# Input loads of a fused convolution and two-layer kernel, split at a multiple of 16 rows

## The chip, the cores and the metric

The kernel runs on one core of a Trainium2 chip. The time is that of the device for one execution, in microseconds (us); where several runs were made, their median is given. The profile is one execution, recorded instruction by instruction, in us from the start of its span.

## What is computed

```python
def _attn_ref(x, weight):
    ...
    w = np.exp(weight - max); w = w / sum          # 8 heads, 7 taps
    x_pad = np.concatenate([zeros(B, 6, D), x], axis=1)
    out = np.einsum('hk,bskhg->bshg', w, x_unf)    # causal 7-tap average, one set of taps per head

def _moe_ref(x, w_in, w_out):
    h = x @ w_in
    g = np.maximum(0.01 * h, h)
    return g @ w_out

def _moe2_ref(x, w_in, w_out, a, b):
    h = x @ w_in
    P = a[0] + a[1]*h + a[2]*h**2 + a[3]*h**3
    Q = 1.0 + abs(b[0])*abs(h) + abs(b[1])*h**2
    return (P / (Q + 1e-06)) @ w_out
```

`x` is 2 x 4096 rows of 192 float32. The convolution's result goes through the first layer (192 to 2048 to 192) and then the second, 8192 rows in all. The four weight matrices arrive as float64 (read as pairs of 32-bit words).

## The kernel before

The 8192 rows are cut into 16 blocks of 512. For each block the kernel loads rows of `x` into one of two tiles `xt` (alternating), forms the convolution on TensorE with banded matrices made of the taps (`conv`), evacuates it to `xc`, transposes it, and splits it in a high and a low part (`xh`, `xl`). Layer 1 runs 16 steps of 128 hidden columns, each with five matrix products into a bank and five into the accumulators `acc`; layer 2 does the same with the rational function between. The two layers of neighbouring blocks are interleaved.

A block is loaded as NTC = 5 overlapping chunks of CR = 109 rows, each 103 rows further on; the last chunk has 106 rows. A row is 768 B. `load_x` issues this as two transfers on SP: L415 takes the full chunks (`109x4x192`), L418 the last (`106x192`). The first block of each half (blocks 0 and 8) begins with six rows of zeros, so its first chunk is a transfer of 103 rows of its own (L411), and L415 has three chunks.

The weights come in 28 pieces through three buffers `raw` (L333, L337 for `w_in`, L339 for `w_out`; 384 or 512 KB each), and each piece is converted by ACT, DVE and POOL from float64 words to a high and a low float32 part. A piece can be loaded only when the piece that had its buffer has been converted: its last reader is `cv_bits`, two `scalar_tensor_tensor` on DVE. Pieces called "m" and "r" belong to `w_in`, those called "o" to `w_out`. The pieces of an "r" kind go through one more pair of SBUF-to-SBUF transfers on SP (`r_dup`, L391).

At the start the taps are normalised on ACT and DVE, stored to DRAM (`s_put`, L302), and read back as bands (`s_get`, L307); DVE and ACT copy them to `band` (L313, L219), and only then can the first convolution run.

The order of all instructions on each engine is fixed when the kernel is built: a planner (`Planner.run`) lists every step with an estimated cost and writes the instructions engine by engine. `load_x` counts there as one step on SP with the cost of three transfers, whatever it issues. All transfers of the kernel, loads, stores (L601) and copies, are issued by SP, in that one order. Each transfer takes the next of eight completion semaphores (`DMAHW0` to `DMAHW7`) in turn, and where its semaphore was used before, it is issued only when that earlier transfer has landed.

The names that the prediction uses: the raw buffers are raw_126, raw_127 and raw_128; "o1" is the second piece of layer 1's `w_out` (in raw_128), "o2" the third (in raw_126).

Of the kernel before, what the change touches and what calls it, by code (L numbers as in the profile page):

```python
# [16 lines left out]
P = 128  # L17
# [139 lines left out]
def conv_leaky_rational_kernel(  # L157
# [12 lines left out]
    nc = tc.nc  # L170
    B, S, D = x.shape
    H, K = weight.shape
# [5 lines left out]
    CT = -(-FB // NTC)  # L178
    CR = CT + K - 1
# [222 lines left out]
        tt(w, buf[("dup", l, q, half)][R:2 * R], f(w), ALU.subtract)  # L402


    def load_x(eng, i):
        b, s0, n, _ = blocks[i]
        t = xt[i % 2]
        ntc = -(-n // CT)
        first = 1 if s0 == 0 else 0
        if first:  # L410
            nc.sync.dma_start(out=t[K - 1:CR, 0, :], in_=x[b, 0:CT, :])  # L411
        r0 = s0 - (K - 1) + first * CT
        src = bass.AP(tensor=x.tensor, offset=x.offset + (b * S + r0) * D,
                      ap=[[D, CR], [CT * D, ntc - 1 - first], [1, D]])
        nc.sync.dma_start(out=t[0:CR, first:ntc - 1, :], in_=src)  # L415
        r0 = s0 - (K - 1) + (ntc - 1) * CT
        rows = n - (ntc - 1) * CT + K - 1
        nc.sync.dma_start(out=t[0:rows, ntc - 1, :], in_=x[b, r0:r0 + rows, :])  # L418

    def zero_x(eng, i):  # L420
        nc.vector.memset(xt[i % 2][0:K - 1, 0, :], 0.0)
# [189 lines left out]
    t1, t2, t = [], [], 0.0  # L611
# [4 lines left out]
    end1, t = t, LEAD  # L616
    for i in range(NB):
        t = max(t, t1[i * NJ + NJ - 1] + GAP)
# [76 lines left out]
    def prep(i):  # L695
        n = blocks[i][2]
        ntc = -(-n // CT)
        p = i % 2
        base = t1[i * NJ]
        c = [base - PREP + STEP * k for k in range(4)] if i else [-77.0] * 4  # L700
        if i >= 2 and blocks[i][1] == 0:
            on(DVE(0.25), base - 66, 2.0, zero_x, i, w=[("xt", p)])
        on(SP(P * ntc * D * 4, 3), max(base - 66, 4) if i else -80, 2.0, load_x, i, w=[("xt", p)], extra=DMA_LAND)
        for m in range(2):
            cps, xps = ("cps", i, m), ("xps", i, m)
            on(PE(0.774), c[m], 2.45, conv, i, m, r=[("xt", p), ("band", m)], w=[cps], take=("bank", cps))
            on(ACT(t_act(ntc * HC) + (m and t_act(ntc * R))), c[m], 4.35, conv_evac, i, m, r=[cps], w=[("xc", m)])
        for m in range(2):
            xps = ("xps", i, m)
            on(PE(0.11 * ntc), c[2 + m], 2.45, trans, i, m, r=[("xc", 0), ("xc", 1), "ident"], w=[xps],  # L710
               take=("bank", xps))
            src = lambda k=xps: buf[k]
            on(ACT(t_act(n)), c[2 + m], 4.35, x_hi, 0, i, m, src, r=[xps], w=[("xh", 0, m, p)])
            on(DVE(t_dve(n)), c[2 + m], 4.36, x_lo, 0, i, m, src, r=[xps, ("xh", 0, m, p)], w=[("xl", 0, m, p)])
# [120 lines left out]
```

## Time and profile before

| | |
|---|---|
| median of 3 runs | 1354.74 us (1353.61 to 1354.93) |
| the profiled execution | 1353.6 us, its span 1351.8 us |
| TensorE (PE) busy | 1268.9 us, 94% |
| ACT busy | 1212.5 us, 90% |
| DVE busy | 1164.5 us, 86% |
| POOL busy | 1160.8 us, 86% |
| mean granted TensorE clock | 0.972 |
| transfers of `x` | 14 of 327 KB and 2 of 245 KB (L415), 16 of 79.5 KB (L418), 2 of 77 KB (L411) |

The span is the time from the first to the last instruction; 1.8 us of the execution lie around it. An engine's busy share is an average over the whole span: the first 160 us, in which the weights are converted, look unlike the rest. A row of the timeline names the engine's idle time ahead of the instruction in square brackets, and what ended it. SPq is SP's issuing of transfers.

### The profile page before, as it was taken

The page shows a single profiled execution, that of the slowest core. Times are in us where ns is not written, and L with a number is a line of the kernel's source. Part 1 is how long each engine was busy: PE and PEld are TensorE (multiplying, and loading weights), DVE is VectorE, ACT ScalarE, POOL GpSimd, SP SyncE. Part 2 cuts the span into 40 slices and gives each one's busy share as a digit, 9 for nine tenths or more (in the row PEclk, how much of TensorE's full clock was granted, in tenths as well). Part 3 has the DMA queues.
Part 4 walks back from the last instruction along what each step waited for, and adds up shares of the span by engine and source line. Part 5 has one row for each costly group of instructions (what it writes and reads, how often), then busy time and mean ns, then how long its engine had stood idle before and what let it go on. Part 6 is the DMA issues. An engine that isn't in the chain of part 4 may idle for free.

```text
span 1351.8 us, 18187 instructions
## 1 busy us (share of the span) xinstructions
PE 1268.9 (94%) x5722; PEld 1024.6 (76%) x5722; DVE 1164.5 (86%) x1784; ACT 1212.5 (90%) x2258; POOL 1160.8 (86%) x934
## 2 busy tenths in 40 slices
PE   4489699999999999999999999999999999999976
PEld 3367578788888878878888887888888787888754
DVE  3399689989989898988989898898989889898996
ACT  2289599999999999999999999999999999999996
POOL 0157499989999899899999989999998998989997
PEclk6689899999999999999999999999999999999997
DMA  4244200000000000000000000000000000000000
GB/s 118 74 126 124 70 4 1 15 10 5 21 1 25 1 24 1 20 5 15 11 1 25 1 25 1 12 1 17 9 13 13 1 25 1 12 1 12 1 13 13
DMA packets 26312, 29.34 MB, mean 22 GB/s; under 512 B 1674, under 2 KB 23654, under 8 KB 26214
## 3 DMA queue, kind: packets, MB, share of 16 engines
q1 hardware_dynamic: 26214, 28.16, 6.8%
q8 instruction: 45, 0.74, 0.2%
q14 instruction: 53, 0.43, 0.1%
HBM read 19.76 MB, written 6.30 MB: 19 GB/s over the span
## 4 chain that ended last, share of the span: by engine, by line
PE 65%; DVE 13%; ACT 11%; SPq 3%; issue 3%; POOL 2%; DMA 2%; ACTq 0%; DVEq 0%; POOLq 0%
PE bank L228 34%; PE acc L228 30%; ACT work L219 7%; SPq L418 3%; DVE work L225 3%; ACT raw L219 3%; DVE work L222 2%; DVE pair L225 2%; DVE bank L225 2%; DVE raw L225 1%; DVE xl L222 1%; DMA raw<-in_moe_w_out_dram 1%; ACT pair L219 1%; PE bank L577 1%; POOL pair L222 1%
## 5 line engine op out<-in xcount | busy, mean ns | idle before, releaser
L228 PE MATMUL acc<-pair,wo 128*128 128x512 f32 x2560 | 670.1, 397 | 29.3 <-ACT pair L219 21.1
L228 PEld LDWEIGHTS acc<-pair,wo 128*128 128x128 f32 x2560 | 475.1, 189 | 137.7 <-ACT pair L219 22.3
L219 ACT ACTIVATE work<-work 128x512 f32<-128x512 f32 x541 | 339.0, 631 | 22.4 <-DVE work L225 16.3
L222 POOL TENSOR_TENSOR pair<-work,pair 128x512 fp32r<-128x512 f32 x196 | 256.1, 1308 | 82.5 <-ACT pair L219 65.0
L222 DVE TENSOR_TENSOR work<-work,bank 128x512 f32<-128x512 f32 (+1 forms) x393 | 253.1, 657 | 16.6 <-ACT work L219 16.6
L219 ACT ACTIVATE work<-bank 128x512 f32<-128x512 f32 (+2 forms) x406 | 226.7, 565 | 9.4 <-PE bank L228 7.7
L228 PE MATMUL bank<-xh,wiH 128*128 128x512 f32 x512 | 207.7, 406 | 26.2 <-DVE work L222 12.9
L222 POOL TENSOR_TENSOR work<-work,pair 128x512 f32<-128x512 f32 x166 | 215.3, 1299 | 14.8 <-DVE pair L225 5.2
L228 PE MATMUL bank<-xh,wiL 128*128 128x512 f32 x512 | 201.4, 393 | 0.0
L228 PE MATMUL bank<-xl,wiH 128*128 128x512 f32 x512 | 201.1, 393 | 0.0
L228 PE MATMUL bank<-xl,wiR 128*128 128x512 f32 x512 | 200.9, 392 | 0.1
L228 PE MATMUL bank<-xh,wiR 128*128 128x512 f32 x512 | 200.8, 392 | 0.0
L219 ACT ACTIVATE raw<-raw 128x512 f32<-128x512 f32 x242 | 151.6, 630 | 7.6 <-DVE raw L225 5.8
L222 POOL TENSOR_TENSOR pair<-work,work 128x512 fp32r<-128x512 f32 x113 | 146.9, 1301 | 11.5 <-DVE work L225 8.0
L225 DVE SCALAR_TENSOR_TENSOR work<-work,b_sb,bank 128x512 f32<-128x512 f32 x166 | 123.5, 744 | 37.9 <-ACT work L219 36.6
L225 DVE SCALAR_TENSOR_TENSOR pair<-bank,a_sb,work 128x512 fp32r<-128x512 f32 x178 | 132.9, 747 | 18.8 <-ACT work L219 14.7
L228 PEld LDWEIGHTS bank<-xh,wiH 128*128 128x128 f32 x512 | 96.9, 189 | 66.6 <-DVE work L222 20.5
L225 DVE SCALAR_TENSOR_TENSOR work<-bank,a_sb,work 128x512 f32<-128x512 f32 x166 | 123.9, 746 | 12.0 <-POOL work L222 11.0
L225 DVE SCALAR_TENSOR_TENSOR bank<-work,a_sb,bank 128x512 f32<-128x512 f32 x175 | 131.5, 752 | 2.8
L219 ACT ACTIVATE pair<-work 128x512 fp32r<-128x512 f32 x196 | 123.6, 631 | 6.1 <-DVE work L222 5.5
L219 ACT ACTIVATE work<-bank,a_sb 128x512 f32<-128x512 f32 x175 | 119.0, 680 | 4.5 <-PE bank L228 3.3
L222 POOL TENSOR_TENSOR raw<-raw,pair 128x512 f32<-128x512 f32 x90 | 116.9, 1300 | 5.6 <-DVE pair L225 1.9
(80 smaller groups left out, 1912.5 us busy)
## 6 DMA issues: line engine op xcount, KB each, us to landing
raw<-in_moe_w_out_dram SPq DMA_DIRECT2D x16, 384.0 KB
xt<-in_x_dram SPq DMA_DIRECT2D x14, 327.0 KB
out_dram<-work SPq DMA_DIRECT2D x22, 192.0 KB
raw<-in_moe_w_in_dram SPq DMA_DIRECT2D x8, 512.0 KB
raw<-in_moe_w_in_dram SPq DMA_DIRECT2D x8, 256.0 KB
work<-work SPq DMA_DIRECT2D x16, 128.0 KB
out_dram<-raw SPq DMA_DIRECT2D x10, 192.0 KB
xt<-in_x_dram SPq DMA_DIRECT2D x16, 79.5 KB
```

Of the source, the lines that this page charges most:

```text
L219: nc.scalar.activation(out=out_, in_=in_, func=func, **k)
L222: (eng or nc.vector).tensor_tensor(out=out_, in0=in0, in1=in1, op=op)
L225: nc.vector.scalar_tensor_tensor(out=out_, in0=in0, scalar=s, in1=in1, op0=op0, op1=op1)
L228: nc.tensor.matmul(out=out_, lhsT=w, rhs=r, start=start, stop=stop)
L418: nc.sync.dma_start(out=t[0:rows, ntc - 1, :], in_=x[b, r0:r0 + rows, :])
L577: nc.tensor.transpose(ps[:, t * P:(t + 1) * P], src[:, t * P:(t + 1) * P], ident)
```

## The change

The full chunks are now loaded with 128 rows each instead of 109 (the 19 further rows are never read by `conv`, which takes rows 0 to 108). The first chunk of blocks 0 and 8 (103 rows) and the last chunk of every block (106 rows) are each split in a transfer of 96 rows and one of the rest, 7 or 10 rows.

```diff
+    def load_rows(t, p0, chunk, src, rows):
+        even = rows - rows % 16
+        for r0, r1 in ((0, even), (even, rows)):
+            if r1 > r0:
+                nc.sync.dma_start(out=t[p0 + r0:p0 + r1, chunk, :], in_=src[r0:r1, :])
+
     def load_x(eng, i):
...
         if first:
-            nc.sync.dma_start(out=t[K - 1:CR, 0, :], in_=x[b, 0:CT, :])
+            load_rows(t, K - 1, 0, x[b, 0:CT, :], CT)
         r0 = s0 - (K - 1) + first * CT
         src = bass.AP(tensor=x.tensor, offset=x.offset + (b * S + r0) * D,
-                      ap=[[D, CR], [CT * D, ntc - 1 - first], [1, D]])
-        nc.sync.dma_start(out=t[0:CR, first:ntc - 1, :], in_=src)
+                      ap=[[D, P], [CT * D, ntc - 1 - first], [1, D]])
+        nc.sync.dma_start(out=t[:, first:ntc - 1, :], in_=src)
         r0 = s0 - (K - 1) + (ntc - 1) * CT
         rows = n - (ntc - 1) * CT + K - 1
-        nc.sync.dma_start(out=t[0:rows, ntc - 1, :], in_=x[b, r0:r0 + rows, :])
+        load_rows(t, 0, ntc - 1, x[b, r0:r0 + rows, :], rows)
```

The instructions on PE, ACT, DVE and POOL stay as they were, in the same order. On SP there are 18 transfers more, and the lines of `load_x` move: L415 is L421 in the changed kernel, and L411 and L418 are L409.

The start of SP's order, up to the storing of the taps. `raw_126` and `raw_127` are the first two weight pieces, `xt_76` is block 0's tile, `work_103` holds the taps:

```order
 L333 DMA raw_126<-in_moe_w_in_dram 128x1024
 L337 DMA raw_127<-in_moe_w_in_dram 64x1024 x2
-L411 DMA xt_76<-in_x_dram 103x192
-L415 DMA xt_76<-in_x_dram 109x3x192
-L418 DMA xt_76<-in_x_dram 106x192
+L409 DMA xt_76<-in_x_dram 96x192
+L409 DMA xt_76<-in_x_dram 7x192
+L421 DMA xt_76<-in_x_dram 128x3x192
+L409 DMA xt_76<-in_x_dram 96x192
+L409 DMA xt_76<-in_x_dram 10x192
 L282 DMA a_sb<-in_moe_a_dram 128x4
 L283 DMA b_sb<-in_moe_b_dram 128x2
```

Three transfers became five, ahead of the same small loads and, behind them, the store of the taps.

That store itself, with the semaphores that its issuing waits for, in the changed kernel on SP:

```order
L282 DMA a_sb<-in_moe_a_dram 128x4 [waits DMAHW1_49]
L283 DMA b_sb<-in_moe_b_dram 128x2 [waits DMAHW2_49]
L302 DMA taps_dram<-work_103 8x256 [waits DMAHW3_49,DVE_49]
L339 DMA raw_128<-in_moe_w_out_dram 128x2x384 [waits DMAHW4_49]
L307 DMA work_106<-taps_dram 128x4x128 [waits DMAHW5_49,DMAHW3_49]
```

Before, the store waited for `DMAHW1`, the load of raw_126; with two more transfers ahead of it, it waits for `DMAHW3`, the second half of the load of raw_127.

Further on in SP's order, where blocks 1 and 2 are loaded (`xt_77`, `xt_76`) between weight pieces; the first `raw_128` is o1, the last `raw_126` is o2:

```order
 L333 DMA raw_127<-in_moe_w_in_dram 128x1024
-L415 DMA xt_77<-in_x_dram 109x4x192
-L418 DMA xt_77<-in_x_dram 106x192
+L421 DMA xt_77<-in_x_dram 128x4x192
+L409 DMA xt_77<-in_x_dram 96x192
+L409 DMA xt_77<-in_x_dram 10x192
 L339 DMA raw_128<-in_moe_w_out_dram 128x2x384
-L415 DMA xt_76<-in_x_dram 109x4x192
-L418 DMA xt_76<-in_x_dram 106x192
+L421 DMA xt_76<-in_x_dram 128x4x192
+L409 DMA xt_76<-in_x_dram 96x192
+L409 DMA xt_76<-in_x_dram 10x192
 L339 DMA raw_126<-in_moe_w_out_dram 128x2x384
```

The weight pieces keep their places behind the loads of `x`; each load of `x` is three transfers instead of two.

## Rows read from the trace of the kernel before

**Rows 1.** The page: engines' busy time, and the chain that ended last

```profile
PE 1268.9 (94%) x5722; PEld 1024.6 (76%) x5722; DVE 1164.5 (86%) x1784; ACT 1212.5 (90%) x2258; POOL 1160.8 (86%) x934
...
PE 65%; DVE 13%; ACT 11%; SPq 3%; issue 3%; POOL 2%; DMA 2%; ACTq 0%; DVEq 0%; POOLq 0%
```

**Rows 2.** Busy by stretch: PE, PEld, DVE, ACT, POOL, granted clock, DMA share, GB/s

```profile
100.00:130.00 30.00, 27.10 (x127) 21.51 (x127) 28.87 (x48) 26.70 (x52) 19.73 (x18) 1.00 0.49 131
...
300.00:500.00 200.00, 199.49 (x920) 163.67 (x919) 181.03 (x275) 190.23 (x356) 188.44 (x149) 1.00 0.04 12
```

**Rows 3.** Chain of waits, first 160 us: start, duration, what

```profile
2.22 5.39 DMA raw<-in_moe_w_in_dram
...
19.27 4.09 DMA taps_dram<-work
...
35.53 7.23 SPq L418
...
45.20 14.83 SPq L418
60.21 7.81 DMA raw<-in_moe_w_out_dram
...
129.05 13.10 SPq L418
142.31 6.78 DMA raw<-in_moe_w_out_dram
...
151.41 2.50 PE bank L228 x5
...
158.54 1.13 PE bank L228 x5
```

**Rows 4.** Tile raw, first 160 us: the engines' idle time by what ended it

```profile
  DMA raw<-in_moe_w_out_dram: 48.0, 4
```

**Rows 5.** Timeline of SP's issuing: start, duration, line, transfer

```profile
4.38 12.48 SPq L418 DMA_DIRECT2D xt<-in_x_dram  x1
...
42.87 1.71 SPq L339 DMA_DIRECT2D raw<-in_moe_w_out_dram  x1
...
83.66 0.37 SPq L339 DMA_DIRECT2D raw<-in_moe_w_out_dram  x1
```

**Rows 6.** Busy by stretch again, for its last two columns, DMA share and GB/s

```profile
12.00:16.80 4.80, 0.00 (x0) 0.00 (x0) 0.53 (x1) 0.00 (x0) 1.15 (x1) 0.61 0.07 23
...
86.60:87.10 0.50, 0.50 (x3) 0.39 (x3) 0.47 (x2) 0.50 (x2) 0.00 (x0) 1.00 0.00 0
```

**Rows 7.** Timeline of ACT and DVE, with idle time before and its releaser

```profile
2.11 0.15 DVE L289 TENSOR_REDUCE red<-wsm 8x1 f32<-8x7 f32 x1 [0.99 <-DMA wsm<-in_weight_dram]
...
27.46 0.43 DVE L313 COPY band<-work 128x512 f32<-128x512 f32 x1 [14.93 <-DMA work<-taps_dram]
...
32.35 0.56 DVE L225 SCALAR_TENSOR_TENSOR work<-bank,work 128x384 int32<-128x384 int32 x1
...
39.44 0.69 DVE L225 SCALAR_TENSOR_TENSOR work<-bank,work 128x512 int32<-128x512 int32 x1
...
49.78 0.54 ACT L219 ACTIVATE work<-raw 128x384 int32<-128x384 uint32 x1 [11.98 <-DMA raw<-in_moe_w_out_dram]
...
51.76 0.57 DVE L356 TENSOR_SCALAR bank<-bank 128x384 f32<-128x384 f32 x1 [10.30 <-ACT bank L219]
...
68.05 0.51 ACT L219 ACTIVATE bank<-raw 128x384 f32<-128x384 f32 x1 [11.84 <-DMA raw<-in_moe_w_out_dram]
...
68.59 0.57 DVE L356 TENSOR_SCALAR bank<-bank 128x384 f32<-128x384 f32 x1 [12.07 <-ACT bank L219]
...
131.62 0.56 DVE L225 SCALAR_TENSOR_TENSOR work<-bank,work 128x384 int32<-128x384 int32 x1
...
149.17 0.51 ACT L219 ACTIVATE bank<-raw 128x384 f32<-128x384 f32 x1 [11.99 <-DMA raw<-in_moe_w_out_dram]
...
150.66 0.69 DVE L222 TENSOR_TENSOR work<-work,bank 128x512 f32<-128x512 f32 x1 [11.24 <-ACT work L219]
```

## The prediction

> **What bounds the kernel now.** The page comes first [rows 1]. PE is busy 94% of the span, and the chain that ended last is PE for 65%; but SPq, the issuing of transfers, holds 3% of it, some 40 us, although SP computes nothing. Second, the stretches [rows 2]: from 300 to 500 us PE is busy 199.49 of 200 us, so whatever comes late before that stretch ends the kernel as much later, and nothing gives it back. From 100 to 130 us DVE is the full engine (28.87 of 30). The loss must lie earlier or between. Third, the chain of the first 160 us [rows 3]: SPq L418, the short load of `x`, stands in it at 35.53, 45.20 and 129.05, each time with a weight load behind it. SP's timeline [rows 5] has a fourth at 4.38: one issue of L418 takes 12.48 us, where L339, for a larger transfer, takes 0.37 us on a free queue. Fourth, ACT [rows 4, 7]: it sat idle 48.0 us for weight pieces, in four waits; three of them are rows of 11.98, 11.84 and 11.99 us. The fourth coincides with DVE's 14.93 us for the taps, whose store stands behind the first L418.
>
> Why L418 holds the queue: while it is being issued, nothing else is in flight, and the DMA engines together are 0.07 busy at 23 GB/s [rows 6]. That is about one engine of sixteen (0.0625). The full chunks (109 rows, 436 pieces of 768 B, 335 KB) seem to lie on one engine: 335 KB at 23 GB/s is 14.6 us, about the time that L418 stays. L418 is where SP stands, not itself the slow transfer. Weight loads with 128 rows do not do that: the one issued at 83.66 has left the DMA engines by 86.6 at the latest, since from there they are idle [rows 5, 6]: 2.9 us for 384 KB.
>
> **The change part by part.** Compute instructions and their order are the same, so the change is SP's four stalls, A to D, and what stood behind each. I take the idle time of DVE, the full engine of this stretch, as the gain, and check each weight load against the moment at which ACT is ready for it.
>
> *A, block 0.* Five issues instead of three, some 0.4 us each as L339 shows [rows 5], end before 6 us. Then a wait is added: the taps' store now waits for the third weight transfer, which landed at 2.22 + 5.39 = 7.61 [rows 3]. Behind it on SP stand the third weight piece and the reading back of the taps; DVE, ACT and PE wait for them. With b_sb's issue in between the store goes out at about 8.0 instead of 19.27. Its landing took 4.09 us behind the clogged engine [rows 3]; a small load on a free queue, the taps' weights, was there at 2.11 after being issued at about 0.7, 1.4 us [rows 7]. Those are the bounds; I take the middle, 2.7, as a store must be confirmed in DRAM. Reading back took from 23.36 to the band copy at 27.46, 4.1 us [rows 3, 7]. So the band copy starts at 8.0 + 2.7 + 4.1 = 14.8: **A gives 12.7 us** (11.3 to 14.0).
>
> *B, block 1.* All times from here are of the old trace; A shifts them together. Without the stall o1 is held by its buffer only: raw_128 is free at 32.35 + 0.56 = 32.9 [rows 7]. ACT was ready for o1 at 49.78 - 11.98 = 37.8. With 2.9 us of transfer o1 is there at 35.8; block 1's `x`, 128 x 4 x 768 B = 393 KB, now on all engines ahead of it, adds as much as another weight piece at most minus what has gone before, and 35.8 + 2.9 = 38.7 would be 0.9 late. With the old 49.78 - 42.87 = 6.9 us it would be 2.0 late. I take no wait: DVE's 10.30 us [rows 7] go. **B gives 10.3.**
>
> *C, block 2.* o2's buffer is free at 39.44 + 0.69 = 40.1 [rows 7]; ACT would be ready at 68.05 - 11.84 - 11.98 = 44.2. Landing after 2.9 us: 43.0, no wait; after the old 7.81 [rows 3]: 47.9, 3.7 late. **C gives DVE's 12.07** [rows 7].
>
> *D, at 129.* The buffer of the held piece is free at 131.62 + 0.56 = 132.2; ACT was ready at 149.17 - 11.99 = 137.2. After 2.9 us: 135.1, in time; after the old 6.78 [rows 3]: 139.0, 1.8 late. **D gives DVE's 11.24** [rows 7]. Behind D, PE is the chain, and after its pause it ran five products in 2.50 us against 1.13 a little later [rows 3]; the granted clock of such a pause is the lower level. That may give up to another 1.4 us per such group of five; it only counts where PE is ahead of the others, and I leave it for the range.
>
> *What is added.* 18 issues of about 0.37 us [rows 5], and 19 x 4 rows of 768 B per block. From block 3 on SP waits for stores and is no bound: the later loads of `x`, which clog the queue alike, are in no chain. I cost that at nothing: the chain's three pieces of L418 [rows 3] make up 35.2 us, most of SPq's 3% [rows 1], so that the eleven later ones cover themselves; were that cover gone, each would cost its issues, some 1.1 us. What is late next is DVE, which is full from C on [rows 2].
>
> Sum: 12.7 + 10.3 + 12.07 + 11.24 = 46.3 us. On the profiled execution, 1353.6, that makes 1307.3; the median of the runs stands 1.1 above it, so **1308.4 us**. Ends: with ACT's three idle times in the place of DVE's (35.8 for 33.6) and A at 14.0, 49.8 us, which is 1304.9; with A at 11.3 and all three weight loads as late as their old landing times make them (2.0 + 3.7 + 1.8), 37.4 us, which is 1317.3.
>
> No row has a transfer of 96 rows; the nearest are those of 128 and of two times 64, which both spread. The Trainium skill (DMA: Bandwidth & Descriptors, section Why a DMA increments its semaphore by 16 and not by 1) says that such a transfer uses as many engines as the largest number up to 16 that divides its slowest dimension: 16 for 96 rows, but 10 and 7 for the rests. By that, the rests are no stall either.
>
> **The rivals.** *1. The rests still hold the queue.* The parts of 7 and 10 rows are no multiple of 16 either. For: the present short load looks slow. Against: it only waits for what is ahead. Price: the first issue behind a held queue took 1.71 against 0.37 us [rows 5], 1.34 more; five such parts stand before the last gain (two in A, one in each of the three other loads before D): 6.7 us, which makes 1315.1. The same skill page (Rules for kernel authors) advises against splitting a transfer by partitions and counts transfers under 64 KB as mostly overhead; its section Anatomy of one DMA gives some 2.0 us fixed for each, on POOL's path. By that the five would cost 10 us in a row, an estimate from that page, and the time would be 1318.4. The trace speaks against a cost in a row: a free queue had taken L339 after 0.37 us, while its bytes moved until 86.6 [rows 5, 6].
>
> *2. The weight loads become the bound.* Three buffers, each reloaded only after its conversion, leave 2.0 (B), 1.2 (C) and 2.1 us (D) of slack at 2.9 us per load. Now `x` moves on the same sixteen engines. For: piece loads beside other traffic took 6.8 to 7.8 us [rows 3]. Against: in those, one engine still had `x` ahead of it. Price: 2.0 + 3.7 + 1.8 = 7.5 us: 1315.9.
>
> *3. Slower.* The row count is not what decides the spread; the overlapping, strided chunks are, and with 128 rows they still lie on one engine. Then 19 x 4 x 768 B = 58 KB more at 23 GB/s [rows 6] lengthens each stall by 2.5 us (block 0's, with three chunks, by 1.9): 9.4 us, 1364.1. It decides if L409 behind L421 is still held for over 10 us. Against: the weights of `w_out` are loaded as 128 x 2 x 384, also three-dimensional, in 2.9 us.
>
> *4. No change.* The other engines wait for something that stands beside L418. Against: four waits, four stalls, and in each the weight load is issued right after L418. 1354.7.
>
> **How the numbers follow.** A measurement of this kernel tells differences over 0.2% from none, 2.7 us here. My forecast with its bounds on landing has 0.75, rivals 1 and 2 have 0.10 and 0.11, rival 3 has 0.02, rival 4 0.02. Faster: 0.96; same 0.02; slower 0.02. The range takes in both ends, 1304.9 and 1317.3, and goes 2 us further on either side for PE's clock after the pauses below and a part of both rivals together above: 1303 to 1320.
>
> **What would show it.** Right: L409 behind L421 issues in under 1 us each, no row of SP over 10 us; the band copy on DVE at about 15 us; ACT's idle time for `raw` under 5 us in place of 48.0; DVE full from 15 to about 95 us; from 200 us on, the same pattern as before. A wrong if the taps land later than 12; B, C or D wrong if ACT still waits over 2 us for a `raw`. The whole is wrong if those waits go and the end does not move: then another engine fills the gaps, and I would look for DVE or PE waits of the same length that are new between 70 and 130 us.

## The result, and the profile after

| | before | the change |
|---|---|---|
| median | 1354.64 us (4 runs, 1353.61 to 1354.93) | 1307.53 us (4 runs, 1304.03 to 1308.70) |
| ratio to before | | 0.9649, 95% interval 0.9630 to 0.9668 |
| the profiled execution, its span | 1353.6, 1351.8 us | 1307.54, 1305.8 us |
| mean granted TensorE clock | 0.972 | 0.993 |

The change is 47.1 us faster by the medians; 46.3 were forecast, and the measured time lies 0.9 us below the forecast 1308.4.

The page's first line of the changed kernel (busy time, share of the span, instructions), against [rows 1]:

```profile
PE 1260.3 (97%) x5722; PEld 1017.4 (78%) x5722; DVE 1165.9 (89%) x1784; ACT 1211.6 (93%) x2258; POOL 1160.0 (89%) x934
```

The work is the same: DVE, ACT and POOL are busy within 1.4 us as long as before, and the span around them is shorter. PE is busy 8.6 us less for the same 5722 products; that goes with its granted clock, whose mean over the first 160 us was 0.81 before and is 0.98 now.

SP's timeline in the changed kernel: start, duration, line, transfer.

```profile
4.29 0.89 SPq L409 DMA_DIRECT2D xt<-in_x_dram  x2
...
8.56 0.30 SPq L302 DMA_DIRECT2D taps_dram<-work  x1
...
9.87 0.93 SPq L307 DMA_DIRECT2D work<-taps_dram  x2
...
18.32 1.09 SPq L409 DMA_DIRECT2D xt<-in_x_dram  x2
19.52 0.39 SPq L339 DMA_DIRECT2D raw<-in_moe_w_out_dram  x1
...
20.47 1.06 SPq L409 DMA_DIRECT2D xt<-in_x_dram  x2
26.84 0.38 SPq L339 DMA_DIRECT2D raw<-in_moe_w_out_dram  x1
...
93.30 0.90 SPq L409 DMA_DIRECT2D xt<-in_x_dram  x2
95.76 0.39 SPq L339 DMA_DIRECT2D raw<-in_moe_w_out_dram  x1
```

Read it against [rows 5]: the two short transfers behind the full chunks issue in 0.9 to 1.1 us together where one stood for 12.48, and the weight loads behind them are no longer held. L339 at 26.84 waits for its buffer (DVE's conversion that frees it ends at 26.78), not for the queue.

DVE's timeline of the changed kernel, at the four places whose counterparts stand in [rows 7] (27.46, 51.76, 68.59, 150.66):

```profile
13.61 0.69 DVE L313 COPY band<-work 128x512 f32<-128x512 f32 x1 [0.21 <-DMA work<-taps_dram]
...
28.75 0.56 DVE L356 TENSOR_SCALAR bank<-bank 128x384 f32<-128x384 f32 x1
...
32.67 0.56 DVE L356 TENSOR_SCALAR bank<-bank 128x384 f32<-128x384 f32 x1
...
103.45 0.68 DVE L222 TENSOR_TENSOR work<-work,bank 128x512 f32<-128x512 f32 x1
```

The same instruction in both traces gives a ruler: it is 13.85, 23.01, 35.92 and 47.21 us earlier. The idle times of 14.93, 10.30, 12.07 and 11.24 us in the brackets of [rows 7] are down to 0.21 us at the first place and gone at the others.

Does that reach the end? The first and the last but one store, SP's timeline, before:

```profile
262.60 0.92 SPq L601 DMA_DIRECT2D out_dram<-work  x2
...
1348.42 0.37 SPq L601 DMA_DIRECT2D out_dram<-raw  x1
```

and in the changed kernel:

```profile
216.42 0.91 SPq L607 DMA_DIRECT2D out_dram<-work  x2
...
1302.17 0.37 SPq L607 DMA_DIRECT2D out_dram<-raw  x1
```

46.18 us at the first, 46.25 at the other: 1.0 us of the 47.2 is given back between 104 and 216 us, and nothing afterwards. Comparing DVE's instructions one by one finds nearly all of it at one place, a pair that writes `wo` (the split weights). DVE and POOL before:

```profile
157.53 1.26 DVE L222 TENSOR_TENSOR wo<-work,wo 128x128 fp32r<-128x128 f32 x2
...
158.64 1.30 POOL L222 TENSOR_TENSOR wiL<-work,wiH 128x512 fp32r<-128x512 f32 x1 [0.34 <-ACT wiH L219]
```

and in the changed kernel:

```profile
110.31 2.39 DVE L222 TENSOR_TENSOR wo<-work,wo 128x128 fp32r<-128x128 f32 x2
...
111.14 1.28 POOL L222 TENSOR_TENSOR wiL<-work,wiH 128x512 fp32r<-128x512 f32 x1
```

The pair takes 2.39 us instead of 1.26, all of it in its second instruction (1.53 for 0.41). In every run of this document that instruction takes 1.53 to 1.55 us where POOL's `wiL` began 0.02 to 0.03 us before it, and 0.41 us where POOL's began 0.27 to 0.84 us after it. That POOL's instruction is what holds DVE fits these times, but was not tested.

The stretches of the changed kernel (PE, PEld, DVE, ACT, POOL, clock, DMA share, GB/s) show which engine is full:

```profile
30.00:60.00 30.00, 26.93 (x125) 19.93 (x123) 29.10 (x50) 26.16 (x52) 20.47 (x22) 1.00 0.45 139
...
300.00:500.00 200.00, 199.68 (x926) 164.48 (x925) 179.54 (x272) 190.38 (x353) 187.92 (x149) 1.00 0.03 9
```

DVE is now full from 30 us on (29.10 of 30; 38.46 of the 40 us behind that), and later PE is (199.68 of 200), as in [rows 2].

What ACT still waits for, by tile `raw` in the first 160 us of the changed kernel, against the 48.0 us of [rows 4]:

```profile
  DMA raw<-in_moe_w_in_dram: 6.4, 4
```

The waits for `w_out` pieces are gone. What is left are four for `w_in` pieces; two of them are here, on ACT's timeline:

```profile
8.57 0.64 ACT L219 ACTIVATE bank<-raw 128x512 f32<-128x512 f32 x1 [1.74 <-DMA raw<-in_moe_w_in_dram]
...
23.20 0.63 ACT L219 ACTIVATE bank<-raw 128x512 f32<-128x512 f32 x1 [1.44 <-DMA raw<-in_moe_w_in_dram]
```

### The profile page after: what moved, and what is told of

The parts are those of the page before. It is cut to its first block, busy times and chain, and to the rows that moved or that the text cites. A ratio compares the mean times of both kernels' runs of the same rounds, so it can differ in the third digit from the quotient of the medians.

```text
span 1305.8 us, 18218 instructions
## 1 busy us (share of the span) xinstructions
PE 1260.3 (97%) x5722; PEld 1017.4 (78%) x5722; DVE 1165.9 (89%) x1784; ACT 1211.6 (93%) x2258; POOL 1160.0 (89%) x934
## 5 line engine op out<-in xcount | busy, mean ns | idle before, releaser
L225 DVE SCALAR_TENSOR_TENSOR work<-bank,a_sb,work 128x512 f32<-128x512 f32 x166 | 123.9, 747 | 11.8 <-POOL work L222 10.6
```

The lines of the kernel that those rows point to most:

```text
L225: nc.vector.scalar_tensor_tensor(out=out_, in0=in0, scalar=s, in1=in1, op0=op0, op1=op1)
```

## The experiments

Eleven kernels ran: four that take the change apart by transfer and row count, four by block, and three beside each other for what is left. All diffs are against the changed kernel.

### Full chunks alone, and split alone

The first keeps the short loads whole:

```diff
-        even = rows - rows % 16
+        even = rows
```

> Full chunks with 128 rows, the short loads (103 and 106 rows) whole. If the full chunks of 109 rows on one engine hold the queue (our theory), nearly the whole gain stays: 1307 to 1311 us; the short loads lie on one or two engines, 79 KB at 23 GB/s is 3.4 us at block 0 and 41 KB per engine 1.8 us at the others, mostly within the slack of the weight loads. If the short load L418 itself is what SP stands at (rival), its 12.5 us issues stay and the time is about 1354 us.

Measured: 1310.75 us, ratio 0.9675 (0.9659 to 0.9692); the kernel before had 1354.95 in this series. As the theory had it. The 3 us to the change come from the start; DVE's timeline of this run:

```profile
18.32 0.43 DVE L313 COPY band<-work 128x512 f32<-128x512 f32 x1 [5.18 <-DMA work<-taps_dram]
```

The band copy is 4.7 us later than in the change, and at the other three places of the ruler DVE is 3.5 us later, no more. The taps' store stood behind the two whole short loads of block 0 (103 and 106 rows): it was issued at 10.20 and the reading back began at 14.30. Which of the two costs how much was not separated.

The second keeps the full chunks at 109 rows:

```diff
-                      ap=[[D, P], [CT * D, ntc - 1 - first], [1, D]])
-        nc.sync.dma_start(out=t[:, first:ntc - 1, :], in_=src)
+                      ap=[[D, CR], [CT * D, ntc - 1 - first], [1, D]])
+        nc.sync.dma_start(out=t[0:CR, first:ntc - 1, :], in_=src)
```

> Short loads split in 96 rows and a rest, full chunks still 109 rows. Theory: the full chunks still lie on one engine, the first short transfer behind them (96 rows) now stands 11 to 13 us, and the time is that of before or up to 5 us more, 1353 to 1360 us. Rival (the short load is the slow one): about 1308 us.

Measured: 1345.46 us, ratio 0.9934 (0.9917 to 0.9950). The rival is out, since SP is still held; but the time is 9.5 us below before, where no gain was expected. SP's timeline of this run:

```profile
4.15 10.29 SPq L409 DMA_DIRECT2D xt<-in_x_dram  x2
...
25.07 13.98 SPq L409 DMA_DIRECT2D xt<-in_x_dram  x2
```

and its waits by tile `raw`, first 160 us:

```profile
  DMA raw<-in_moe_w_out_dram: 39.4, 4
```

The queue is held about as long as before at blocks 1 to 3 (13.98 us at block 1, where L418 stood for 13.59) and 2.2 us less at block 0, yet ACT's four waits are 8.6 us shorter. Splitting took rows off the engine with the backlog: block 0's first chunk put 103 x 768 B = 79 KB on it, 3.4 us at 23 GB/s, and each short load of 106 rows half of its rows, 41 KB or 1.8 us (the DMA share of a 106-row load is below). 3.4 + 4 x 1.8 = 10.6 us, an estimate, for 9.5 measured. The weight load behind the queue shows it; o1 in this run, SP's and ACT's timeline:

```profile
39.16 0.38 SPq L339 DMA_DIRECT2D raw<-in_moe_w_out_dram  x1
...
44.02 0.55 ACT L219 ACTIVATE work<-raw 128x384 int32<-128x384 uint32 x1 [10.51 <-DMA raw<-in_moe_w_out_dram]
```

From the issue to ACT's start it is 4.86 us here and 6.91 before (42.87 and 49.78 in [rows 5, 7]); for o2 it is 5.73 for 7.84, for D's piece 5.06 for 6.86. So each lands about 2 us sooner, as the 1.8 had it. What stands behind the queue in time is not the issue of L418 alone, but the backlog that it adds to: the later weight load lands behind it.

The two gains, 44 and 9.5 us, sum to more than 47: both shorten the same four waits.

### Which row counts spread

Full chunks with 110 rows, and with 113, instead of 128:

```diff
-                      ap=[[D, P], [CT * D, ntc - 1 - first], [1, D]])
-        nc.sync.dma_start(out=t[:, first:ntc - 1, :], in_=src)
+                      ap=[[D, 110], [CT * D, ntc - 1 - first], [1, D]])
+        nc.sync.dma_start(out=t[0:110, first:ntc - 1, :], in_=src)
```

> Full chunks with 110 rows, one more than the kernel before loads; the short loads split as in the change. If what counts is a common factor of the row count with the number of engines used (110 can be dealt to 11 or 10 engines evenly), the DMA share during such a load is about 0.6 to 0.7, SP is not held, and the time is 1306 to 1311 us. If only multiples of 16, or full 128 rows, spread, the load goes to one or two engines and the time is 1340 to 1358 us.

> Full chunks with 113 rows, a prime number, otherwise the change. If the row count's factors decide, all 452 pieces lie on one engine: SP is held as before, somewhat longer (4 x 4 x 768 B at 23 GB/s is 0.5 us per load), 1354 to 1360 us. If any load of over some row count spreads, or the split of the short loads is what matters, about 1308 us.

Measured: 1309.45 us with 110 rows, ratio 0.9667 (0.9648 to 0.9686); 1347.52 with 113, ratio 0.9948 (0.9928 to 0.9968). One row more than before gives nearly the whole gain (45.5 us), three more than that take most of it back. The run with 113 rows came out 6.5 us below its expected range, for the same reason as the split alone: its short loads are split, too. Against that run it is 2.1 us slower, about the 0.5 us per stall that 4 x 4 more rows were to cost.

The stretches of a later load of `x` (the last two columns are DMA share and GB/s), where little else is in flight. 113 rows:

```profile
261.00:270.00 9.00, 9.00 (x42) 7.45 (x41) 8.53 (x13) 8.32 (x16) 8.92 (x8) 1.00 0.07 23
```

The short load of 106 rows, in the run with full chunks alone:

```profile
225.00:226.00 1.00, 1.00 (x6) 0.84 (x5) 0.78 (x2) 1.00 (x3) 1.00 (x2) 1.00 0.12 40
```

110 rows:

```profile
222.00:222.50 0.50, 0.50 (x4) 0.42 (x3) 0.50 (x1) 0.50 (x3) 0.50 (x2) 1.00 0.73 238
```

128 rows, in the change:

```profile
219.50:220.00 0.50, 0.50 (x4) 0.41 (x3) 0.47 (x2) 0.50 (x2) 0.50 (x1) 1.00 1.03 347
```

Divide the first three by the last: 0.07, 0.12 and 0.71, which is one, two and eleven engines of sixteen (0.06, 0.125, 0.69). The eleven hang on one row: the two half microseconds before it show 0.75 and 0.83, with the split short load perhaps still moving beside the full chunks. The Trainium skill (DMA: Bandwidth & Descriptors, section Why a DMA increments its semaphore by 16 and not by 1) says that the number of engines is the largest up to 16 that divides the slowest dimension of both sides: 1 for 113, 2 for 106, 11 for 110. These rows agree.

### Block by block

The change for some blocks, the loads of the others as before; the condition is `i == 0`, `i <= 1`, `i <= 3` and `i >= 4`:

```diff
+        new = i == 0
+        wide = P if new else CR
...
-        even = rows - rows % 16
+        even = rows - rows % 16 if new else rows
...
-                      ap=[[D, P], [CT * D, ntc - 1 - first], [1, D]])
-        nc.sync.dma_start(out=t[:, first:ntc - 1, :], in_=src)
+                      ap=[[D, wide], [CT * D, ntc - 1 - first], [1, D]])
+        nc.sync.dma_start(out=t[0:wide, first:ntc - 1, :], in_=src)
```

> The change for block 0 alone, the loads of all other blocks as before. Theory: the four stalls are independent and add up, and block 0's is worth what the trace of the change shows at the band copy, 27.46 - 13.61 = 13.9 us (forecast as 12.7): 1340 to 1343 us. Rival, that the stalls behind it take part of that back since their loads wait for the queue anyway: 1345 to 1354 us.

> The change for blocks 0 and 1. Theory: 13.9 us and B's 9 to 10: 1330 to 1333 us. Rival, that o1's earlier load only lets ACT reach the third stall sooner, so that C's wait grows by as much: 1339 to 1343 us, the time of block 0 alone.

> The change for blocks 0 to 3, the loads of blocks 4 to 15 as before. Theory: the four stalls are all of it, and the later loads, which hold the queue as long, cover themselves: 1306 to 1310 us, no different from the change. Rival, that the later ones cost something by the stores behind them: up to 12 x 0.5 us more, 1311 to 1316 us.

> The reverse: blocks 0 to 3 as before, the change from block 4 on. Theory: no gain that can be told, 1352 to 1356 us. Rival: 1340 to 1350 us.

| changed blocks | median, us | ratio to before | gain, us |
|---|---|---|---|
| 0 | 1342.88 | 0.9912 (0.9892 to 0.9932) | 11.8 |
| 0 and 1 | 1329.56 | 0.9814 (0.9794 to 0.9834) | 25.1 |
| 0 to 3 | 1307.41 | 0.9647 (0.9631 to 0.9663) | 47.3 |
| 4 to 15 | 1354.55 | 1.0001 (0.9991 to 1.0011) | 0.1 |

The four stalls are all of it. Step by step A gives 11.8, B 13.3, C and D together 22.2; that these sum to the whole lies in how the runs are nested, and C and D were not separated. Nor are A and B quite separable. In the run with block 0 alone, DVE's timeline has

```profile
13.17 0.53 DVE L313 COPY band<-work 128x512 f32<-128x512 f32 x1 [0.37 <-DMA work<-taps_dram]
...
41.13 0.57 DVE L356 TENSOR_SCALAR bank<-bank 128x384 f32<-128x384 f32 x1 [13.46 <-ACT bank L219]
```

The band copy is 14.3 us early, but the wait at block 1 has grown from 10.30 us [rows 7] to 13.46. So part of A goes into B's stall as long as that is there. With blocks 0 and 1 changed the time came out 0.4 us below the expected 1330 to 1333.

That later loads cover themselves can be seen directly. SP's timeline of the run with blocks 0 to 3 changed:

```profile
107.50 12.73 SPq L409 DMA_DIRECT2D xt<-in_x_dram  x1
...
218.68 12.39 SPq L409 DMA_DIRECT2D xt<-in_x_dram  x1
```

Blocks 4 and on hold the queue for 12 us as ever, and the time is that of the change. With blocks 4 to 15 alone changed, ACT's waits by tile `raw` stay as in [rows 4]:

```profile
  DMA raw<-in_moe_w_out_dram: 49.5, 4
```

### What is left

The change again, and two ways to go further. One transfer per block, with 128 rows for the last chunk too (blocks 0 and 8 keep the two of their first chunk, the last block all three):

```diff
+        full = ntc if i + 1 < NB else ntc - 1
...
-                      ap=[[D, P], [CT * D, ntc - 1 - first], [1, D]])
-        nc.sync.dma_start(out=t[:, first:ntc - 1, :], in_=src)
+                      ap=[[D, P], [CT * D, full - first], [1, D]])
+        nc.sync.dma_start(out=t[:, first:full, :], in_=src)
+        if full == ntc:
+            return
```

and block 0's load of `x` issued behind the taps' store, by naming the taps as something that the load waits for in the planner:

```diff
-        on(SP(P * ntc * D * 4, 3), max(base - 66, 4) if i else -80, 2.0, load_x, i, w=[("xt", p)], extra=DMA_LAND)
+        on(SP(P * ntc * D * 4, 3), max(base - 66, 4) if i else -80, 2.0, load_x, i, r=[] if i else ["taps"],
+           w=[("xt", p)], extra=DMA_LAND)
```

> The change itself once more, beside the next two on the same chip: 1305 to 1309 us.

> The last chunk is loaded with 128 rows in the same transfer as the full chunks (its rows past 106 belong to later rows of x and reach no output), so a block is one transfer of 128 x 5 rows instead of three; the last block of all keeps the three. Theory: transfers on free engines are in no chain after block 0, and the time is that of the change within 2 us, 1304 to 1309 us. Rival, that the two small transfers cost the weight loads behind them some 2 us each at four places, or the stores behind them: 1297 to 1303 us.

> Block 0's load of x is issued behind the store of the taps and the third weight piece instead of ahead of them; order and kind of all compute instructions stay. In the change the band copy waited only 0.21 us, but ACT waited 1.74 us for the second weight piece, which shared the engines with x, and the store went out at 8.56. Theory: the band copy starts 1 to 2.5 us sooner (11 to 12.6 us) and DVE, full from there on, carries this to the end: 1303 to 1307 us. Rival: the first convolution then waits for x itself, and nothing or a loss results: 1306 to 1311 us.

Measured, five runs each: 1307.24 us, ratio 0.9649 (0.9636 to 0.9663); 1308.55, ratio 0.9657 (0.9644 to 0.9671); 1306.98, ratio 0.9651 (0.9638 to 0.9664). The three cannot be told apart, so no version beats the change. The last lies in both of its expected ranges, so its time does not decide between them.

One transfer instead of three gains nothing. The Trainium skill (DMA: Bandwidth & Descriptors, section Rules for kernel authors) advises one transfer of 128 partitions rather than several to parts of them. Here that holds in so far as the split has no merit of its own over a load of 128 rows; against leaving 103 and 106 rows whole it was worth some 3 us (1310.75 against 1307.53). The 10 us that the forecast had worked out from that page's 2.0 us per transfer (section Anatomy of one DMA) are not there: without four of the five rests the time is the same.

The later load of `x` did what it was to do, and it is worth following where that went. DVE's timeline of that run:

```profile
12.59 0.98 DVE L313 COPY band<-work 128x512 f32<-128x512 f32 x1
...
31.87 0.57 DVE L356 TENSOR_SCALAR bank<-bank 128x384 f32<-128x384 f32 x1
...
89.67 0.63 DVE L222 TENSOR_TENSOR wo<-work,wo 128x128 fp32r<-128x128 f32 x2 [1.17 <-ACT wo L219]
90.22 0.56 DVE L356 TENSOR_SCALAR bank<-bank 128x384 f32<-128x384 f32 x1
```

The band copy is 1.0 us earlier than in the change, and 0.8 us are still there at the clip of o2 (31.87 for 32.67). At 89.67 DVE waits 1.17 us for ACT. The row at 90.22 has a counterpart in the change, on DVE's timeline, with nothing won:

```profile
90.09 0.55 DVE L356 TENSOR_SCALAR bank<-bank 128x384 f32<-128x384 f32 x1
```

ACT's timeline of the later-load run names what made ACT late:

```profile
84.00 0.60 ACT L219 ACTIVATE work<-bank 128x512 f32<-128x512 f32 x1 [0.91 <-POOL pair L222]
```

By the profile ACT waited there for an instruction of POOL. The change itself has no such wait at this place. It is not the planner edge that makes it, though: the run with 110 rows, which has none, shows it as well, on ACT's timeline:

```profile
85.81 0.60 ACT L219 ACTIVATE work<-bank 128x512 f32<-128x512 f32 x1 [0.89 <-POOL pair L222]
```

So do the runs with one transfer per block (0.71 us) and with blocks 0 and 1 changed (0.91 us). What in the timing brings it about was not looked into.

## Why the prediction was right, step by step

- *What bounds the kernel.* Right: four stalls of SP, all in the first 160 us. The runs by block show it (47.3 us from blocks 0 to 3, 0.1 from the others). The step from "later loads of `x` are in no chain" to "they cost nothing" held although they hold the queue just as long.
- *Why L418 holds the queue.* Right in the main: the full chunks lie on one engine, and 110 against 113 rows show that the count of rows decides. Why one more issue has to stand while an engine has that backlog, no run here shows. Too narrow in one point: "L418 is where SP stands, not itself the slow transfer". It lies on two engines, and it and block 0's first chunk are worth 9.5 us alone.
- *A, forecast 12.7:* 13.85 at the band copy. Three of its terms were off: the third weight transfer did not land at 7.61 but let ACT start at 8.57, since `x` now shares its engines (with `x` issued later, in the last run, ACT starts at 7.84), and the store went out at 8.56 for the forecast 8.0; its landing took at most 1.3 us (8.56 to 9.87) for the 2.7 that I took, near the lower bound of 1.4; reading back took 3.7 for 4.1. So 0.6 lost against 1.4 and 0.4 won. The middle between the two bounds was chosen because this was a store; it took no longer than the small load.
- *B, forecast 10.3:* 9.16 (23.01 - 13.85). The wait for o1 went; but the piece before it came late, which no step of the forecast had looked at (ACT's 1.44 us at 23.20).
- *C, forecast 12.07:* 12.91, as a wait of 0.65 us that DVE had for ACT shortly before (at 55.83) went with it. *D, forecast 11.24:* 11.29. Loads land before ACT is ready for them, as the slack of 1 to 2 us had said. That slack was larger than the forecast took it: only the first of the two `scalar_tensor_tensor` of a conversion reads `raw`, so a buffer is free some 0.6 us sooner. The loads of o2 and of D's piece were issued at 26.84 and 95.76, right behind the ends of that first one at 26.78 and 95.70.
- *The sum*, 46.3, stood against 47.2 at the last of the four places and 46.2 from the first store on. That it came so close is in part luck: the parts missed by 1.15 (A) and 0.84 (C) too little and 1.14 (B) too much, and the 1.0 us given back behind them, at one pair of DVE's instructions, was not forecast.
- *What is added.* The later loads that cost nothing are twelve, not eleven, as block 3's is D itself.
- *The rivals.* The rests hold nothing (0.9 to 1.1 us for two issues). The weight loads did not become the bound; ACT's wait for them is 6.4 us, a little over the "under 5" that I had named as a sign, and 3.7 us of such waits for `w_in` were there before the change as the first two pieces landed. The overlapping chunks spread, so the slower case fell. One more sign was off: DVE is not full from 15 us on, but 7.45 of the 10 us up to 25.
- PE's clock after the pauses, which I had left for the range, did not show as a further gain. Behind D's pause, in which PE was busy 2.19 of 12 us, the granted clock was 0.50, the lower level, from 150 to 155 us; in the change it is 1.00 there (100 to 110 us), and D's 11.29 is DVE's wait and no more.

## What to carry to other kernels

Look at the share of the DMA engines while a queue is held: 0.07 or 0.12 of sixteen engines says that a transfer lies on one or two of them, and the row count of the load is the first thing to check. Here 110 rows in place of 109 were worth nearly as much as 128, and splitting the short loads gained nothing over loading 128 rows. Price such a stall by what stands behind it in the same queue: the first four loads of `x` were worth 47 us, since weight loads stood behind them, the next twelve nothing. And when stalls sit in a row, compare the same instruction in both traces at each of them, since a stall that remains takes back part of what the one before it gave.

## What the runs showed that was not expected

A load that was dealt to few engines hurt twice here: SP stood until most of the backlog had drained, and the next weight load landed behind what was left. Taking 79 KB and four times 41 KB off that engine gave 9.5 us although the queue was held for 10 to 15 us all the same. And small losses come and go behind a large gain: one pair of DVE's instructions took 1.1 us longer, or ACT waited 0.9 us for POOL, in some runs and not in others, with the same compute instructions in the same order.
